# Storing the split of layer one's output weights in DRAM in the second chunk and loading it from there in chunks three to five

## The chip, the cores and the metric

The kernel runs on one core of a Trainium2 chip. The metric is the device time of one execution in microseconds, over the whole kernel from the first instruction to the last output; several runs are taken and their median is quoted.

## What is computed

Three stages, one after the other, in float32 (the sizes are those of the kernel):

```
attention: B, H, S, D = 4, 8, 576, 64, causal window of 128, a linear bias per head
    attn = softmax(q k^T / sqrt(D) + bias, masked);  x = attn v        -> x is (2304, 512)
layer one: d_ff = 1536
    g = x @ w_gate;  val = x @ w_val
    x = (g * sigmoid(g) * val) @ w_out                                  -> (2304, 512)
layer two: d_ff = 2048
    h = x @ w_in
    y = (h * tanh(softplus(h))) @ w_out                                 -> (2304, 512)
```

The weights of the two layers arrive as raw 64-bit words and are converted to float32 on the chip.

## The kernel before

**Products.** TensorE multiplies in a rounded float32 type. To keep accuracy most operands are split into a rounded part and what is left of it, here called the halves: ScalarE writes the rounded copy (`hi_act`, L123), VectorE the difference (`lo_dve`, L126). A product then takes three matmuls: high by high, high by low, low by high. All matmuls go through `mm` (L116).

**Tokens.** The 2304 tokens of attention and layer one run in five chunks, `A_CHUNKS = [512, 384, 512, 512, 384]`, called `ci` = 0 to 4 in the code and first to fifth in this text. While TensorE computes layer one of a chunk, the attention of the next one is woven in piece by piece. The order on TensorE is the program's order; on the other engines and on SP, whose queue issues nearly all the transfers, a scheduler that models the time sets the order when the kernel is built.

**Layer one.** For each of 12 blocks `i` of 128 hidden features, `gv_groups` computes gate and value (24 matmuls into `g_ps`, operands `xt` and `w`) and splits the result into `hh` and `hl`; `out_group` then adds the block's product with the output weights (12 matmuls into four accumulators `acc`, through `proj`). The output product of a block runs one block after its gate and value; in the fifth chunk it lags six blocks (`lastlag`), so the last seven blocks' output products follow each other directly at the end of layer one.

**The ring.** The output weights of two blocks, 128 x 1024 numbers, make one piece `r` (six pieces for a chunk). In use it lies as halves, 128 x 2 x 1024, in a `ring` tile; there are two such tiles (`ring_tile`, `bufs=2`). The first chunk converts the raw words (`conv_ring`) and writes the float32 weights to DRAM (`w1od`). For every later chunk `load_ring(ci, r)` is called when the output product of the piece two before it has been issued, so that the tile just used can be filled again. It puts four steps at the front of the list `bg` of background steps: load 512 KB from `w1od` into a `cw` tile, an empty step, ScalarE's high half and VectorE's low half. `pump` takes a few steps from that list after each group of TensorE's work, and `need` forces those that are due.

**Other background work on the same list.** `conv_w2` converts layer two's 16 weight blocks in the second to fourth chunk (raw words into the one `wraw` tile; ScalarE's L434 makes `cg`; VectorE's L446, L439, L451 and L460 make `cw`; then a store to `w2d`). In the fifth chunk `combos` loads eight of these blocks from `w2d` (`cw`), forms differences on GpSimd (`ct`, L577), splits them into `chl` and writes them to `w2o` (16 stores). `make_win` prepares layer two's input weights (`w` from `w2d`, differences `t` on GpSimd at L850, halves `win`).

**Layer two.** It runs three times over 768 tokens: products into `bk` from `xs` and `win`, then from `op` and `wout` (loads of 1024 KB from `w2o`).

Of the kernel before, what the change touches and what calls it, by code (L numbers as in the profile page):

```python
# [9 lines left out]
F32 = mybir.dt.float32  # L10
# [12 lines left out]
NF1, NF2 = F1 // 128, F2 // 128  # L23
# [70 lines left out]
def body(ctx: ExitStack, tc: tile.TileContext, qT, kT, vP, w1, w1o, w2, cst, yT):  # L94
    nc = tc.nc
# [6 lines left out]
    dr = ctx.enter_context(tc.tile_pool(name="dr", bufs=1, space=bass.MemoryType.DRAM))  # L102
# [2 lines left out]
    x2d = dr.tile([128, CT, NT], F32, name="x2d")  # L105
    w1od = dr.tile([NF1 // 2, 128, 1024], F32, name="w1od")
    w2d = dr.tile([NF2, 128, 1024], F32, name="w2d")
    w2o = dr.tile([7, 128, NJ, 2, 256], F32, name="w2o")
    cst_sb = const.tile([128, 452], F32, name="cst_sb")
    nb = {128: cst_sb[:, 0:128], 0: cst_sb[:, 128:256]}  # L110
# [290 lines left out]
    wt, ring, spill = {}, {}, {}  # L401
    bg = collections.deque()
    done = set()
# [16 lines left out]
    def steps(key, fs, front=False):  # L420
        if front:
            bg.extendleft([(key if f is fs[-1] else None, f) for f in fs][::-1])
            return
        for f in fs[:-1]:
            bg.append((None, f))
        bg.append((key, fs[-1]))
# [39 lines left out]
    def halves(st, alloc, put):  # L466
        def f1():
            st["h"] = alloc()
            hi_act(st["h"][:, 0], st["w"])

        def f2():
            lo_dve(st["h"][:, 1], st["w"], st["h"][:, 0])
            put(st["h"])

        return [f1, f2]

    def ring_tile():
        return hp_.tile([128, 2, 1024], F32R, tag="ring", name="ring", bufs=2)
# [46 lines left out]
        )  # L525

    def load_ring(ci, r):
        st = {}

        def f0():  # L530
            st["w"] = hp_.tile([128, 1024], F32, tag="cw", name="cw")
            nc.sync.dma_start(out=st["w"], in_=w1od[r])

        def put(w):
            ring[ci, r] = w

        steps(
            ("ring", ci, r), [f0, lambda: None] + halves(st, ring_tile, put), True
        )
# [177 lines left out]
    def out_group(ci, i):  # L717
        p = plansA[ci]

        def o():  # L720
            acc = get_acc(("A", ci))
            hh, hl = hs.pop(("A", ci, i))
            r, j = divmod(i, 2)
            need(("ring", ci, r))
            proj(acc, p.n, ring[ci, r], 512 * j, hh, hl, i == 0, i == NF1 - 1)
            if j == 1:
                ring.pop((ci, r))
                if ci == 0 and r + 2 < NF1 // 2:
                    conv_ring(r + 2)
                else:  # L730
                    nxt = (ci, r + 2) if r + 2 < NF1 // 2 else (ci + 1, r + 2 - NF1 // 2)
                    if nxt[0] < len(plansA):
                        load_ring(*nxt)
            if i == NF1 - 1:
                with tc.high_priority(CFG["evprio"]):
                    evacuate(acc, p.n, x2d[:, :, p.t0:p.t0 + p.n])

        return [o]
# [439 lines left out]
```

## Time and profile before

| | us |
|---|---|
| median of 3 runs (lowest, highest) | 941.27 (940.84, 942.20) |
| the execution that was profiled | 940.25 |
| its span, first to last instruction | 938.4 |
| TensorE busy in it | 917.4 (98%) |
| VectorE, ScalarE, GpSimd busy | 698.2, 518.1, 198.5 |

The profiled execution's own time is its span and 1.85 us around it; it lies 1.02 us under the median. "Busy" of TensorE is the time in which at least one matmul was in its pipeline; the row of weight loads (PEld) runs beside it. A row of the timeline gives the start, the length, the engine, the line, what is written from what, and in brackets how long the engine sat idle before it and what ended that.

### The profile page before, as it was taken

The page shows a single profiled execution, that of the slowest core. Times are in us where ns is not written, and L with a number is a line of the kernel's source. Part 1 is how long each engine was busy: PE and PEld are TensorE (multiplying, and loading weights), DVE is VectorE, ACT ScalarE, POOL GpSimd, SP SyncE. Part 2 cuts the span into 40 slices and gives each one's busy share as a digit, 9 for nine tenths or more (in the row PEclk, how much of TensorE's full clock was granted, in tenths as well). Part 3 has the DMA queues.
Part 4 walks back from the last instruction along what each step waited for, and adds up shares of the span by engine and source line. Part 5 has one row for each costly group of instructions (what it writes and reads, how often), then busy time and mean ns, then how long its engine had stood idle before and what let it go on. Part 6 is the DMA issues. An engine that isn't in the chain of part 4 may idle for free. (4 is left out here: it accounts for less than half of the span.)

```text
span 938.4 us, 14535 instructions
## 1 busy us (share of the span) xinstructions
PE 917.4 (98%) x5016; PEld 820.8 (87%) x5016; DVE 698.2 (74%) x1333; ACT 518.1 (55%) x1127; POOL 198.5 (21%) x332
## 2 busy tenths in 40 slices
PE   5999999999999999999999999999999999999998
PEld 4765678898998888888878999999999999999998
DVE  6898996677866776477664896678976789766874
ACT  6865667656675755355433554564645545455442
POOL 1312132110210332001012455451012410131000
PEclk9999999999999999999999999999999999999999
DMA  9855443366636554164427986625793257930375
GB/s 350 293 216 180 146 125 101 104 212 202 207 106 183 193 175 160 32 208 156 155 100 269 375 292 216 227 90 187 262 299 113 82 187 261 308 119 2 105 260 195
DMA packets 76729, 174.86 MB, mean 186 GB/s; under 512 B 8944, under 2 KB 52336, under 8 KB 66928
## 3 DMA queue, kind: packets, MB, share of 16 engines
q1 hardware_dynamic: 76512, 173.67, 56.1%
q8 instruction: 40, 0.66, 0.3%
q14 instruction: 33, 0.27, 0.1%
q10 hardware_dynamic: 144, 0.26, 0.1%
HBM read 138.25 MB, written 35.65 MB: 185 GB/s over the span
## 5 line engine op out<-in xcount | busy, mean ns | idle before, releaser
L116 PE MATMUL g_ps<-xt,w 128*128 128x512 f32 (+1 forms) x1440 | 318.3, 373 | 0.0
L116 PEld LDWEIGHTS g_ps<-xt,w 128*128 128x128 f32 x1440 | 257.6, 188 | 36.7 <-issue 3.5
L116 PE MATMUL bk<-xs,win 128*128 128x384 f32 x1008 | 175.8, 334 | 1.3 <-DVE G L759 1.0
L116 PE MATMUL bk<-op,wout 128*128 128x384 f32 x1008 | 175.8, 334 | 0.9 <-DMA wout<-w2o 0.8
L116 PEld LDWEIGHTS bk<-xs,win 128*128 128x128 f32 x1008 | 174.7, 188 | 1.9 <-DVE G L759 1.3
L116 PEld LDWEIGHTS bk<-op,wout 128*128 128x128 f32 x1008 | 174.8, 188 | 1.5 <-issue 1.5
L116 PE MATMUL acc<-hh,ring 128*128 128x512 f32 (+1 forms) x432 | 132.3, 369 | 0.1
L123 ACT ACTIVATE op<-G 128x768 fp32r<-128x768 f32 x84 | 71.1, 847 | 64.3 <-PE bk L116 54.4
L280 POOL TENSOR_SCALAR_AFFINE_SELECT PT<-PT 128x256 f32<-128x256 f32 (+4 forms) x80 | 44.2, 568 | 232.2 <-ACT PT L277 232.0
L126 DVE TENSOR_TENSOR op<-G,op 128x768 fp32r<-128x768 f32 x84 | 79.5, 957 | 15.8 <-ACT op L123 15.0
L116 PEld LDWEIGHTS acc<-hh,ring 128*128 128x128 f32 x432 | 80.0, 188 | 10.0 <-DVE ring L126 0.4
L850 POOL TENSOR_TENSOR t<-w 128x256 f32<-128x256 f32 x48 | 40.2, 858 | 209.6 <-DVE win L126 146.7
L116 PE MATMUL acc<-hl,ring 128*128 128x512 f32 (+1 forms) x216 | 79.0, 366 | 0.0
L759 DVE TENSOR_TENSOR G<-u,bk 128x384 f32<-128x384 f32 x72 | 39.7, 553 | 41.4 <-PE bk L116 39.8
L249 ACT ACTIVATE Pt<-Pt,sm 128x128 f32<-128x128 f32 (+1 forms) x160 | 62.3, 391 | 14.0 <-DVE sm L245 13.3
L686 ACT ACTIVATE t<-g_ps 128x512 f32<-128x512 f32 (+1 forms) x60 | 32.9, 548 | 48.5 <-PE g_ps L116 48.3
L123 ACT ACTIVATE hh<-t 128x512 fp32r<-128x512 f32 (+1 forms) x54 | 31.3, 579 | 45.3 <-DVE t L702 45.1
L687 DVE SCALAR_TENSOR_TENSOR t<-t,g_ps 128x512 f32<-128x512 f32 (+1 forms) x60 | 37.6, 627 | 22.9 <-ACT t L686 22.9
L1122 ACT ACTIVATE G<-G 128x384 f32<-128x384 f32 x72 | 37.2, 517 | 29.0 <-DVE G L759 29.0
L264 ACT ACTIVATE Pt<-Pt,sm 128x128 f32<-128x128 f32 (+1 forms) x144 | 46.3, 391 | 9.2 <-DVE sm L260 9.0
L702 DVE SCALAR_TENSOR_TENSOR t<-t,g_ps 128x512 f32<-128x512 f32 (+1 forms) x54 | 33.6, 623 | 20.1 <-PE g_ps L116 19.1
L126 DVE TENSOR_TENSOR hl<-t,hh 128x512 fp32r<-128x512 f32 (+1 forms) x54 | 36.5, 676 | 16.0 <-ACT hh L123 15.2
(84 smaller groups left out, 1266.9 us busy)
## 6 DMA issues: line engine op xcount, KB each, us to landing
wout<-w2o SPq DMA_DIRECT2D x42, 1024.0 KB, 5.9
wraw<-w SPq DMA_DIRECT2D x16, 1024.0 KB, 5.5
w2o<-chl SPq DMA_DIRECT2D x16, 896.0 KB, 8.8
wst<-w SPq DMA_DIRECT2D x12, 1024.0 KB, 7.8
cw<-w1od SPq DMA_DIRECT2D x24, 512.0 KB, 4.5
w<-w2d SPq DMA_DIRECT2D x24, 512.0 KB, 3.5
w2d<-cw SPq DMA_DIRECT2D x16, 512.0 KB, 4.7
wraw<-w1o SPq DMA_DIRECT2D x6, 1024.0 KB, 6.8
```

What stands on the lines that cost most here:

```text
L116: nc.tensor.matmul(out=out, lhsT=lhsT, rhs=rhs, start=start, stop=stop, skip_group_check=True)
L123: return nc.scalar.activation(out=out, in_=in_, func=AF.Copy)
L126: return nc.vector.tensor_tensor(out=out, in0=in_, in1=hi.bitcast(F32), op=ALU.subtract)
L249: last_of["sum"] = nc.scalar.activation(out=Pt[:q.qn], in_=Pt[:q.qn], func=AF.Exp, scale=-1.0, bias=sm[:q.qn, i:i + 1], accum_out=sm[:q.qn ...
L264: last_of["exp"] = nc.scalar.activation(out=pt, in_=pt, func=AF.Copy, scale=r)
L280: nc.gpsimd.affine_select(out=here, in_=prev, pattern=[[0, m], [1, n]], compare_op=ALU.is_ge, fill=0.0, base=0, channel_multiplier=-1,)
L686: tanhs.append(nc.scalar.activation(out=t[:, :n], in_=st["g"][:, :n], func=AF.Tanh, scale=0.5))
L687: nc.vector.scalar_tensor_tensor(out=t[:, :n], in0=t[:, :n], scalar=1.0, in1=st["g"][:, :n], op0=ALU.add, op1=ALU.mult)
L702: nc.vector.scalar_tensor_tensor(out=t[:, :n], in0=t[:, :n], scalar=0.5, in1=vps[:, :n], op0=ALU.mult, op1=ALU.mult)
L759: last_of["add"] = nc.vector.tensor_tensor(out=out, in0=a, in1=b, op=op)
L850: nc.gpsimd.tensor_tensor(out=x[:, o], in0=a, in1=b, op=ALU.subtract)
L1122: nc.scalar.activation(out=out, in_=in_, func=AF.Mish)
```

## The change

`load_ring` of the second chunk also stores each piece's halves to a new DRAM tensor `w1oh` (six stores of 1024 KB), right after VectorE has written the low half. For the third to fifth chunk `load_ring` no longer adds steps to the list: it takes a `ring` tile and issues one load of 1024 KB from `w1oh` straight into it, and ScalarE and VectorE split nothing. Line numbers behind the new lines are 1, 6 or 7 higher.

```diff
@@ -105,6 +105,7 @@
     x2d = dr.tile([128, CT, NT], F32, name="x2d")
     w1od = dr.tile([NF1 // 2, 128, 1024], F32, name="w1od")
     w2d = dr.tile([NF2, 128, 1024], F32, name="w2d")
+    w1oh = dr.tile([NF1 // 2, 128, 2, 1024], F32, name="w1oh")
     w2o = dr.tile([7, 128, NJ, 2, 256], F32, name="w2o")
@@ -525,6 +526,11 @@
     def load_ring(ci, r):
+        if ci >= 2:
+            ring[ci, r] = ring_tile()
+            nc.sync.dma_start(out=ring[ci, r].bitcast(F32), in_=w1oh[r])
+            done.add(("ring", ci, r))
+            return
         st = {}
 
         def f0():
@@ -533,6 +539,7 @@
 
         def put(w):
             ring[ci, r] = w
+            nc.sync.dma_start(out=w1oh[r], in_=w.bitcast(F32))
 
         steps(
             ("ring", ci, r), [f0, lambda: None] + halves(st, ring_tile, put), True
```

The scheduler's order on TensorE and on GpSimd is the same in both kernels. The order moves on SP, ScalarE and VectorE, from the second chunk to the end of layer one. Two places of it follow.

**SP, the end of the fifth chunk, before.** `cw<-w1od` are the old loads of the output weights, `cw_...<-w2d` and `w2o<-chl` the loads and stores of `combos`, `w_...<-w2d` the weights for `make_win`, `x2d<-ev` the results of layer one.

```order
L612 DMA w2o<-chl 128x7x256 x2
L532 DMA cw<-w1od 128x1024
L588 DMA cw_5839<-w2d 128x1024
L612 DMA w2o<-chl 128x7x256
L843 DMA w_5854<-w2d 128x1024
L612 DMA w2o<-chl 128x7x256 x2
L532 DMA cw<-w1od 128x1024
L612 DMA w2o<-chl 128x7x256
L843 DMA w_5905<-w2d 128x1024
L612 DMA w2o<-chl 128x7x256
L666 DMA x2d<-ev 128x2x384 x2
```

The last two loads of output weights stand ahead of five and of two of the sixteen `w2o` stores.

SP, the same stretch, with the change:

```order
L531 DMA ring<-w1oh 128x2048
L619 DMA w2o<-chl 128x7x256
L595 DMA cw_5749<-w2d 128x1024
L619 DMA w2o<-chl 128x7x256 x2
L531 DMA ring<-w1oh 128x2048
L850 DMA w_5816<-w2d 128x1024
L619 DMA w2o<-chl 128x7x256 x2
L850 DMA w_5867<-w2d 128x1024
L619 DMA w2o<-chl 128x7x256
L531 DMA ring<-w1oh 128x2048 x2
L673 DMA x2d<-ev 128x2x384 x2
```

Each load into `ring` now waits for TensorE to be done with the tile, so it stands where that comes: the third piece behind ten stores, the fourth behind thirteen, the fifth and sixth together behind all sixteen.

**ScalarE, the middle of the second chunk, before.** `cg<-wraw` is the conversion of a weight block that has to be loaded first; `K` and `Q` are the split of the next head's keys and queries, `ring<-cw` the high half of an output weight piece.

```order
L686 ACTIVATE t<-g_ps 128x384
L249 ACTIVATE Pt,sm<-Pt,sm 128x128 x2
L434 ACTIVATE cg<-wraw 128x1024
L123 ACTIVATE K_2518<-kraw 128x640
L203 ACTIVATE Q<-qraw 128x512
L123 ACTIVATE hh<-t 128x384
L249 ACTIVATE Pt,sm<-Pt,sm 128x128 x2
L123 ACTIVATE ring<-cw 128x1024
L277 ACTIVATE PT<-t_ps 128x4x128
```

The conversion stands ahead of `K` and `Q`.

ScalarE, the same place, with the change:

```order
L693 ACTIVATE t<-g_ps 128x384
L250 ACTIVATE Pt,sm<-Pt,sm 128x128 x2
L124 ACTIVATE K_2523<-kraw 128x640
L204 ACTIVATE Q<-qraw 128x512
L124 ACTIVATE hh<-t 128x384
L250 ACTIVATE Pt,sm<-Pt,sm 128x128 x2
L278 ACTIVATE PT<-t_ps 128x4x128
L265 ACTIVATE Pt<-Pt,sm 128x128 x4
L435 ACTIVATE cg<-wraw 128x1024
```

`K` and `Q` stand ahead of the conversion now.

## Rows read from the trace of the kernel before

**Rows 1.** The page's head and its busy times by engine.
```profile
span 938.4 us, 14535 instructions
PE 917.4 (98%) x5016; PEld 820.8 (87%) x5016; DVE 698.2 (74%) x1333; ACT 518.1 (55%) x1127; POOL 198.5 (21%) x332
```

**Rows 2.** Busy times by stretch: second, third, fourth, fifth chunk, layer two.
```profile
core 0: us, PE busy (x) PEld busy (x) DVE busy (x) ACT busy (x) POOL busy (x), PEclk, DMA share, GB/s
183.00:285.00 102.00, 100.26 (x637) 94.39 (x636) 76.00 (x194) 66.33 (x183) 17.89 (x38) 1.00 0.62 188
285.00:405.00 120.00, 120.00 (x635) 97.58 (x634) 78.21 (x190) 67.15 (x188) 23.21 (x56) 1.00 0.48 150
405.00:512.00 107.00, 107.00 (x535) 87.36 (x534) 69.29 (x131) 49.36 (x104) 13.84 (x22) 1.00 0.51 167
512.00:584.00 72.00, 71.63 (x411) 70.98 (x410) 59.59 (x70) 37.84 (x55) 35.36 (x36) 1.00 0.86 300
584.00:937.00 353.00, 349.15 (x2009) 347.93 (x2008) 264.26 (x353) 175.24 (x272) 66.16 (x85) 1.00 0.54 181
```

**Rows 3.** What TensorE waited for from 100 us on: total, times, longest.
```profile
PE s_ps L116 <- DVE Q L205: 3.2, 4, 1.3
PE bk L116 <- DVE G L759: 1.0, 1, 1.0
PE bk L116 <- DMA wout<-w2o: 0.8, 1, 0.8
PE bk L116 <- DVE ev L665: 0.3, 1, 0.3
```

**Rows 4.** All instructions that write `ring`: ns shortest, median, longest.
```profile
L123 ACT ACTIVATE ring<-cw x27: 1042/1057/1064, 98.6 to 574.6; 128x1024 fp32r<-128x1024 f32 x27
L126 DVE TENSOR_TENSOR ring<-cw,ring x27: 1184/1226/1760, 99.7 to 576.0; 128x1024 fp32r<-128x1024 f32 x27
```

**Rows 5.** Timelines of the second chunk: SP, ScalarE, VectorE, TensorE.
```profile
223.53 0.38 SPq L491 DMA_DIRECT2D wraw<-w  x1
...
230.30 1.13 ACT L434 ACTIVATE cg<-wraw 128x1024 bf16<-128x1024 bf16 x1 [3.08 <-DMA wraw<-w]
231.33 0.72 ACT L123 ACTIVATE K<-kraw 128x640 fp32r<-128x640 f32 x1
...
232.94 0.69 DVE L205 SCALAR_TENSOR_TENSOR Q<-qraw,Q 64x512 fp32r<-64x512 f32 x1
...
233.69 0.38 PE L116 MATMUL s_ps<-K,Q 128*128 128x256 f32 x1 [1.35 <-DVE Q L205]
```

**Rows 6.** TensorE's timeline, fifth chunk: output products, then layer two.
```profile
535.76 0.35 PE L116 MATMUL acc<-hh,ring 128*128 128x384 f32 x1
542.03 0.35 PE L116 MATMUL acc<-hh,ring 128*128 128x384 f32 x1
567.10 0.35 PE L116 MATMUL acc<-hh,ring 128*128 128x384 f32 x1
573.53 0.34 PE L116 MATMUL acc<-hl,ring 128*128 128x384 f32 x1
573.97 0.62 PE L116 MATMUL acc<-hh,ring 128*128 128x384 f32 x2
581.89 0.34 PE L116 MATMUL acc<-hh,ring 128*128 128x384 f32 x1
583.55 34.60 PE L116 MATMUL bk<-xs,win 128*128 128x384 f32 x198 [0.27 <-DVE ev L665]
```

**Rows 7.** ScalarE's and VectorE's timelines: splits of single pieces, fourth and fifth chunk.
```profile
494.20 1.06 ACT L123 ACTIVATE ring<-cw 128x1024 fp32r<-128x1024 f32 x1 [0.99 <-PE acc L116]
...
572.22 1.69 DVE L126 TENSOR_TENSOR ring<-cw,ring 128x1024 fp32r<-128x1024 f32 x1
```

**Rows 8.** Issue to landing of loads of 1024 KB: all of `wout`, all of `wraw`.
```profile
DMA to landing us min/median/max: 4.9/5.9/10.0
DMA to landing us min/median/max: 4.7/5.6/8.8
```

**Rows 9.** Transfers by stretch, KB each, median us to landing: 520 to 540, 556 to 570.
```profile
w2o<-chl SPq DMA_DIRECT2D x5, 896.0 KB, 10.5
w2o<-chl SPq DMA_DIRECT2D x4, 896.0 KB, 7.0
```

**Rows 10.** SP's timeline, end of the fourth chunk and of the fifth.
```profile
492.35 1.26 SPq L588 DMA_DIRECT2D cw<-w2d  x2
...
569.59 0.36 SPq L612 DMA_DIRECT2D w2o<-chl  x1
```

## The prediction

> **What bounds the kernel now.** I read the page's head first, then busy times by stretch, then TensorE's waits, then the timelines at the few places where it waits. TensorE is busy 98% of the span [rows 1]. By stretch the point is sharper: in the third and fourth chunk, 285 to 512 us, it is busy for every microsecond, in the fifth chunk for 71.63 of 72, in the second for 100.26 of 102, always at the full granted clock of 1.00 [rows 2], which is the upper of its two levels. VectorE has free time in all of them: the length less its busy time is 26, 42, 38 and 12 us from the second to the fifth chunk, and ScalarE has more [rows 2]. From 100 us on TensorE lost 5.3 us to named waits [rows 3]: 3.2 for queries that VectorE split late (attention), 0.3 for the results of layer one being copied out, 1.0 and 0.8 in layer two. The kernel is TensorE's work end to end, and the change takes no matmul away: 5016 before, in the same order after. So it can gain only what lies in these waits and can lose wherever a new wait on TensorE appears.
>
> **The change part by part.**
>
> *The splits removed.* Of 27 splits of a piece [rows 4] the change leaves nine (three in the first chunk, six in the second). 18 go: 18 x 1.06 = 19 us of ScalarE and 18 x 1.23 = 22 us of VectorE. Between 285 and 512 us TensorE has no wait that this could end, so twelve of the 18 are worth nothing there. The matmuls are the cover; if it were gone the most would be the 22 us.
>
> *The loads doubled.* 18 loads of 512 KB become 18 of 1024 KB, 9 MB more over some 300 us where the transfers' share is 0.48, 0.51 and 0.86 [rows 2]. The price of one is that of the nearest row of equal size and direction: 5.9 us in the median for `wout`, 5.6 for `wraw`, 4.7 at the least and 10.0 at the most [rows 8]. The load cannot start before TensorE has finished with the tile, since the halves go straight into it; before, only the splits waited for the tile and the 512 KB had been fetched ahead. So each load has the time of one piece's use, two output products and what lies between. In the fifth chunk two such products start 6.27 us apart, at 535.76 and 542.03 [rows 6], so a tile has 12.5 us, and 10.0 fits. In the chunks with 512 columns it has more. These loads cost nothing, with the other tile's work as cover.
>
> *The end of the fifth chunk is the exception.* There seven output products run back to back: 84 matmuls from 567.10 to 582.06 [rows 6], which is the last one's start at 581.89 and the 0.17 that one takes, less the pause at 573.97, which is 2.10 us for a product and 4.2 for a piece. The third piece is used up with the first of the seven, at 569.2; the fifth piece's load can start then, and TensorE wants it two products on, at 573.4. Before, the splits took 1.06 and 1.7 us there and ended only a little late: TensorE paused 0.26 us, from 573.71 to 573.97, for a low half that VectorE wrote from 572.22 to 573.91 [rows 6, 7]. Now a load has to land in those 4.2 us, less the wake-up of SP and that of TensorE: from the end of that split to TensorE's start it was 0.06 us, and twice that is 0.1 (an estimate). So TensorE waits for the landing time less about 4.0. At 4.7 that is 0.7, at 10.0 it is 6.0. I take 5.9, since `wout` is the same shape on the same route: **1.9 us**. The median is nearer than the slow end, because the last `w2o` stores should be out before this load: SP issued the sixteenth at 569.59 [rows 10], with three splits fewer ahead of it on VectorE, and landings late in the chunk have come down from 10.5 to 7.0 [rows 9]. The sixth piece's load starts at 573.4, lands at 579.4 by the same row, and is wanted at 573.4 + 1.9 + 4.2 = 579.5: no second wait at that landing time.
>
> The Trainium skill, "DMA: Bandwidth & Descriptors", section "Anatomy of one DMA — SWDGE (gpsimd) path", fits a transfer as 2.0 us and the bytes at 436 GB/s, so 1 MiB in 4.4 us (an estimate from that page, whose fit is for another issuing path than SP's). By it the wait would be 0.4 us and the kernel 1.5 us faster than in my sum; the fastest such load here took 4.7 [rows 8], so I stay with the rows.
>
> *Waits that go there.* The 0.26 us pause goes with its split, and the wait of 0.27 us at 583.55 for VectorE's copies [rows 6] goes too, since VectorE has two splits less ahead of them while TensorE arrives later. Together −0.5.
>
> *The steps taken off the list.* Each of the 18 loads took four steps of the list; without them the conversion of layer two's weights comes earlier in chunks three and four, where neither engine is full. Nothing for TensorE. At the end of the fourth chunk SP now has three loads into `ring` in a row, and the first two loads of `combos` stand behind them. The third of these waits for a tile that TensorE let go at 494.2 [rows 7], so `combos` starts near 494.5 where it started at 492.35 [rows 10], 2.2 us later, bounded below by 0 and above by the 10.0 of one landing. VectorE's 12 us of room in the fifth chunk and six splits less (7 us) take that up by 569 us; if not, see the first rival.
>
> *SP's queue.* A load that waits for TensorE holds all that stands behind it. In the fifth chunk that is, behind the third piece's load, the last `combos` load and two stores; behind the fourth's, two loads for `make_win`; behind the last two, only results that TensorE has not yet computed. All were issued at about these times before, so I put it at nothing, with 2 us for the first of them at the most, the same 2.2 as above.
>
> *The stores in the second chunk.* Six stores of 1024 KB, 6 MB more in 102 us where the transfers' share is 0.62 [rows 2] at 188 GB/s: some 60 GB/s more, share about 0.8. The issue of one takes SP 0.4 us, in front of loads of keys, queries and raw words. Nothing waits for the stores themselves before the third chunk. The price is what they delay.
>
> *The order in the second chunk.* The largest single wait for queries, 1.35 us at 233.69, has its cause on ScalarE: the conversion at 230.30 sat 3.08 us for raw words that SP had asked for at 223.53, and `K` and `Q` stood behind it, so VectorE ended `Q` at 233.6 [rows 5]. With the change `K` and `Q` stand ahead of the conversion, so the wait goes: **−1.35**. Later raw words, by up to the 3 us between the 5.6 and the 8.8 of [rows 8], then hold up a conversion and no query. The bound above is 0 (another head takes its place), the one below −1.7, with all the waits there.
>
> *The sum.* +1.9 − 0.5 − 1.35 = +0.05, so 940.3 on the profiled execution's 940.25. That execution lies 1.02 under the median; on the median's scale it is **941.3**.
>
> **What a measurement tells.** 0.2% is 1.9 us, about what a measurement of this kernel can tell from no change. The forecast is no change.
>
> **The rivals.**
>
> *A crowded landing at the end (slower).* Place: the load of the fifth piece at 569 us. With 9 to 10 us, as loads have it beside others [rows 8, 9], TensorE waits 5 to 6 instead of 1.9 and the kernel takes 944.4 to 945.4. It gets there too if `combos` runs late, since that load stands behind the sixteenth store on SP and every microsecond of that store past 569.2 is one of TensorE. It decides from a landing of 7.7 us on, with the second chunk's gain, or 6.4 without. For it: the share of 0.86 and the three engines' chain in `combos`. Against: the last stores had been issued by 569.59 even with the splits in the way. Chance 0.22.
>
> *The stores crowd the second chunk (slower).* 6 MB more delay the loads of queries and keys, and the 3.2 us of waits for queries grow instead of shrinking. If the 1.35 stays and doubles, the kernel is at 941.3 + 2.7 = 944.0. Against: a share of 0.62 leaves room, and queries are loaded a head ahead. Chance 0.06.
>
> *Relief everywhere (faster).* The last load lands at 4.7, which costs 0.7, all 1.7 of the second chunk's waits for queries go, and the 1.0 that TensorE waits for VectorE in layer two goes [rows 3], with two splits less ahead of layer two's weights: 0.7 − 0.5 − 1.7 − 1.0 = −2.5, 938.8. Against: that wait hangs on a chain that starts from TensorE's own products and moves with it. Chance 0.12.
>
> *The change does not do what it says.* If the new loads waited for the last of the six stores, or were not early in any chunk, TensorE would show waits at every piece, 15 times (landing minus room). The rows of SP show each load into `ring` right where its tile comes free, so I give this no chance of its own beyond the range's edge, 0.02, slower.
>
> **How the numbers follow.** Forecast 0.58; the rivals 0.22, 0.06, 0.12 and 0.02. Slower by over 0.2%: 0.22 + 0.06 + 0.02 = 0.30, of which some lie just inside, so 0.28. Faster 0.12. Within: 0.60. The range runs from 939.5, the forecast with the full 1.7 gained and a landing of 4.7 (1.6 under it), to 945.0, inside the first rival; left out are about half of the faster rival and a third of the slower ones, under 2 in 10.
>
> **What would show it.** Right: 18 splits less, nine left in the rows of `ring`; no wait of TensorE between 285 and 560 us; one new wait, on a transfer into `ring`, of 1 to 3 us near 573 us; the wait for `Q` near 233 us gone; layer two as before, shifted by a microsecond at most. Wrong: waits for `ring` in other places, two of them at the end, a wait for `Q` that has grown, or TensorE held at the start of layer two by `win`.

## The result and the profile after

| | before | after |
|---|---|---|
| median, us (lowest, highest), 4 runs each side by side | 941.74 (940.84, 942.62) | 953.55 (953.31, 955.21) |
| ratio to before, 95% interval | | 1.0124 [1.0102, 1.0145] |
| span of the profiled execution, us | 938.4 | 951.6 |

The change costs 11.8 us. The forecast was 941.3 with a range from 939.5 to 945.0, so the result lies far outside, on the side of the slower rivals and beyond the price of each. The two profiled executions took 940.25 and 953.31, so the traces have 13.1 us to explain and not 11.8.

The page of the kernel after, its head and its busy times by engine, against [rows 1]:

```profile
span 951.6 us, 14475 instructions
PE 920.7 (97%) x5016; PEld 823.3 (87%) x5016; DVE 675.1 (71%) x1315; ACT 502.9 (53%) x1109; POOL 192.1 (20%) x332
```

The 18 splits are gone from both engines: VectorE has 23.1 us less to do, ScalarE 15.2. TensorE has the same 5016 matmuls, and the span is 13.2 us longer. Busy times by stretch in the kernel after, as in [rows 2]:

```profile
core 0: us, PE busy (x) PEld busy (x) DVE busy (x) ACT busy (x) POOL busy (x), PEclk, DMA share, GB/s
183.00:285.00 102.00, 99.61 (x632) 93.79 (x631) 74.73 (x193) 65.38 (x179) 15.31 (x36) 1.00 0.76 243
285.00:405.00 120.00, 116.74 (x617) 94.60 (x617) 67.56 (x175) 59.72 (x175) 15.74 (x59) 1.00 0.52 166
405.00:512.00 107.00, 105.95 (x528) 85.69 (x527) 61.24 (x128) 43.52 (x102) 13.31 (x18) 1.00 0.57 190
512.00:584.00 72.00, 67.66 (x385) 66.87 (x384) 54.27 (x68) 34.60 (x53) 36.30 (x37) 0.99 1.03 358
584.00:937.00 353.00, 351.18 (x2006) 350.25 (x2006) 262.01 (x348) 175.81 (x275) 69.36 (x88) 0.99 0.54 178
```

The third and fourth chunk, where TensorE was busy for every microsecond, now have holes of 3.3 and 1.1 us, although both other engines have less to do there. The fifth has one of 4.3, and its mean granted clock is 0.99. TensorE's waits from 100 us on, against [rows 3] (total, times, longest):

```profile
PE s_ps L117 <- DVE Q L206: 5.6, 6, 1.4
PE acc L117 <- DMA ring<-w1oh: 4.3, 1, 4.3
PE o_ps L117 <- issue: 1.9, 1, 1.9
PE bk L117 <- DMA wout<-w2o: 1.3, 2, 0.8
PE bk L117 <- DVE G L766: 1.0, 1, 1.0
PE g_ps L117 <- DVE sm L246: 0.7, 1, 0.7
```

Matmul for matmul, both traces have the same order on TensorE, so the start of the same matmul can be subtracted. This ledger, worked out from the two traces, is where the 13.2 us of the spans went; "lag" is after minus before:

| where, us in before | first matmul that is later | change of the lag | lag then |
|---|---|---|---|
| second chunk, 208.75, 233.69, 257.90 | `s_ps<-K,Q` | +1.12, -1.41, +0.95 | 0.68 |
| third chunk, 321.41 | `o_ps<-PT,v` | +1.94 | 2.62 |
| third chunk, 345.11, 345.57 | `s_ps<-K,Q`, `g_ps<-xt,w` | +0.85, +0.98 | 4.44 |
| fourth chunk, 435.02 | `s_ps<-K,Q` | +1.31 | 5.75 |
| fifth chunk, 573.36 | `acc<-hh,ring`, the fifth piece | +4.60 | 10.35 |
| 573.53 to 576.86 | its next matmuls, at half the clock | +2.4 | 12.74 |
| start of layer two, 583.55 | `bk<-xs,win` | -0.33 | 12.41 |
| layer two, 928.59 | `bk<-op,wout` | +0.57 | 12.98 |

Two losses hold 12.1 of the 13.2 us: 5.1 in the third and fourth chunk, 7.0 at the end of the fifth. They have different causes. The rest is +0.7 in the second chunk, where the forecast had -1.35, and small changes in layer two.

**The third and fourth chunk.** The conversion of layer two's weights runs closer together. The rows of the `wraw` tile from 285 to 512 us; first the kernel before (of one instruction: shortest, median, longest ns, then first and last start; then what its engines waited for: us, times; then the landings), second the kernel after, where `DVE cw L447` is of those that waited for the tile:

```profile
L446 DVE TENSOR_SCALAR cw<-wraw x11: 684/692/778, 293.2 to 488.3; 128x1024 int32<-128x1024 int32 x11
...
  DMA wraw<-w: 16.6, 8
...
DMA to landing us min/median/max: 4.9/5.3/6.1
```

```profile
L447 DVE TENSOR_SCALAR cw<-wraw x11: 694/694/718, 285.4 to 451.9; 128x1024 int32<-128x1024 int32 x11
...
  DMA wraw<-w: 30.6, 14
...
  DVE cw L447: 10.0, 7
...
DMA to landing us min/median/max: 5.1/6.6/9.4
```

Of eleven passes the last starts at 452 us instead of 488. There is one tile for raw words, so the next load starts only when the passes before it are over; closer passes wait more often, 14 times instead of 8, and now on VectorE too, 10.0 us in seven waits, where it had none. What such a wait does to TensorE shows at 321 us. From the timelines of SP, ScalarE, VectorE and TensorE of the kernel after, with the wait ahead of an instruction in brackets:

```profile
310.53 0.33 SPq L492 DMA_DIRECT2D wraw<-w  x1
...
319.49 1.15 ACT L435 ACTIVATE cg<-wraw 128x1024 bf16<-128x1024 bf16 x1 [3.93 <-DMA wraw<-w]
...
319.50 0.69 DVE L447 TENSOR_SCALAR cw<-wraw 128x1024 int32<-128x1024 int32 x1 [4.05 <-DMA kraw<-kT]
...
323.25 0.68 DVE L694 SCALAR_TENSOR_TENSOR t<-t,g_ps 128x512 f32<-128x512 f32 x1
...
324.03 1.75 PE L117 MATMUL o_ps<-PT,v 128*64 128x256 f32 x24 [1.87 <-issue]
```

Both engines stand for 4 us before a pass whose words SP had asked for at 310.53, 9.0 us earlier. (For VectorE's wait the page names a load of keys, which this pass does not read; ScalarE's pass on the same words starts 0.01 us before it.) The work that stands behind the pass on VectorE comes late, among it the product that reads a `g_ps` bank; it ends at 323.93, and 0.10 later TensorE starts the matmuls that need a bank. The page can name no releaser for this wait. (That the bank is what TensorE waited for is read from these times, and was not tried apart.)

**The end of the fifth chunk.** SP's timeline and TensorE's in the kernel after:

```profile
566.50 5.47 SPq L619 DMA_DIRECT2D w2o<-chl  x2
572.13 0.44 SPq L850 DMA_DIRECT2D w<-w2d  x1
572.85 0.86 SPq L619 DMA_DIRECT2D w2o<-chl  x1
575.24 4.50 SPq L531 DMA_DIRECT2D ring<-w1oh  x2
```

```profile
583.71 0.66 PE L117 MATMUL acc<-hh,ring 128*128 128x384 f32 x1 [4.34 <-DMA ring<-w1oh]
584.16 0.52 PE L117 MATMUL acc<-hl,ring 128*128 128x384 f32 x1
...
589.88 0.34 PE L117 MATMUL acc<-hl,ring 128*128 128x384 f32 x1
590.05 0.51 PE L117 MATMUL acc<-hh,ring 128*128 128x384 f32 x2
```

The load of the fifth piece is issued at 575.24, as soon as TensorE has left the tile; TensorE has used up the piece between at 583.71 - 4.34 = 579.37, 4.13 us later. The load's landing time is the longest of the three after 560 us:

```profile
DMA to landing us min/median/max: 6.7/7.3/8.3
```

8.3 less 4.1 is the wait, to 0.2 us. The landing belongs to its stretch: the same loads in the same kernel took 5.3 us in the median between 285 and 512 us, where the transfers' share is 0.52 and 0.57, and 8.3 between 512 and 560. Of the last three `w2o` stores, asked for at 566.50, 571.59 and 572.85, two were still under way at 575.24, the last until 581.86. (That these stores are what slowed the load was not tried apart.)

Then the clock falls; busy times and granted clock in three stretches around it:

```profile
570.00:580.00 10.00, 9.37 (x54) 9.05 (x53) 7.45 (x9) 7.09 (x9) 5.05 (x6) 1.00 1.06 368
580.00:590.00 10.00, 6.29 (x20) 6.32 (x21) 2.65 (x2) 1.06 (x1) 7.08 (x8) 0.66 0.53 209
590.00:600.00 10.00, 10.00 (x60) 10.00 (x59) 2.78 (x5) 1.48 (x3) 0.00 (x0) 1.00 0.47 142
```

From 583.7 to about 589.9 matmuls start 0.32 us apart instead of 0.17, the lower of the two levels of the clock: 2.4 us more.

### The profile page after: what moved, and what is told of

It reads as the page before. It is cut to its first block, busy times and chain, and to the rows that moved or that the text cites. A ratio compares the mean times of both kernels' runs of the same rounds, so it can differ in the third digit from the quotient of the medians.

```text
span 951.6 us, 14475 instructions
## 1 busy us (share of the span) xinstructions
PE 920.7 (97%) x5016; PEld 823.3 (87%) x5016; DVE 675.1 (71%) x1315; ACT 502.9 (53%) x1109; POOL 192.1 (20%) x332
## 4 chain that ended last, share of the span: by engine, by line
PE 78%; DVE 8%; DMA 8%; issue 2%; SPq 2%; ACT 1%; POOL 1%; DVEq 0%; ACTq 0%; POOLq 0%
PE bk L117 34%; PE g_ps L117 25%; PE acc L117 13%; PE s_ps L117 3%; PE o_ps L117 3%; DMA wraw<-w 2%; DMA wout<-w2o 2%; PE t_ps L272 1%; DVE cw L452 1%; DMA v<-vP 1%; DVE Pt L246 1%; DMA ring<-w1oh 1%; DVE cw L447 1%; POOL t L857 1%; SPq L189 1%
## 5 line engine op out<-in xcount | busy, mean ns | idle before, releaser
L117 PE MATMUL acc<-hh,ring 128*128 128x512 f32 (+1 forms) x432 | 134.5, 374 | 4.3 <-DMA ring<-w1oh 4.3
L281 POOL TENSOR_SCALAR_AFFINE_SELECT PT<-PT 128x256 f32<-128x256 f32 (+4 forms) x80 | 39.1, 505 | 238.2 <-ACT PT L278 238.0
```

The source lines that it names most:

```text
L117: nc.tensor.matmul(out=out, lhsT=lhsT, rhs=rhs, start=start, stop=stop, skip_group_check=True)
L281: nc.gpsimd.affine_select(out=here, in_=prev, pattern=[[0, m], [1, n]], compare_op=ALU.is_ge, fill=0.0, base=0, channel_multiplier=-1,)
```

## The experiments

Each ratio is to runs of the kernel before on the same chip in the same session (their medians were 940.2 to 942.4; the changed kernel's own is in the section above). Parts of a loss are read from the ledger of each kernel against the profile of before, made as above. The runs of one kernel scatter by 2 to 9 us, so single profiles can begin a few microseconds late; only the change of the lag inside a stretch is used.

**1. Stores alone.** All chunks load and split as before.

```diff
-        if ci >= 2:
+        if ci >= 5:
...
-            nc.sync.dma_start(out=w1oh[r], in_=w.bitcast(F32))
+            if ci == 1:
+                nc.sync.dma_start(out=w1oh[r], in_=w.bitcast(F32))
```

> Only the six stores of the halves in the second chunk are added to the kernel before; every chunk loads the words and splits them as before, so the list of steps is as it was. Theory 'stores crowd the second chunk': the new waits there (+1.3 near 209 us, +0.9 near 258) come with the stores, the wait at 233.7 goes only if the order on ScalarE changes too; 941.5 to 944. Rival 'all of the second chunk's shift is order': no change, 941.2 to 942.2, and the wait of 1.35 at 233.7 stays.

Measured: 941.36, ratio 1.0016 [1.0000, 1.0032]. The lag changes by +1.58 at 208.75, -1.41 at 233.69 and -0.65 at 257.90; the third to fifth chunk are as before. So the first two moves of the second chunk come with the stores, the gain forecast at 233.69 among them, and nearly cancel. The rival's time holds, its reason (the wait at 233.69 stays) doesn't; of the first theory's two new waits the one near 209 us comes and the one near 258 doesn't.

**2. The list's steps put back.**

```diff
-            done.add(("ring", ci, r))
+            steps(("ring", ci, r), [lambda: None] * 4, True)
```

> Each direct load leaves four empty steps at the head of the list of background steps, as many as the old load had; loads, stores and computation are the changed kernel's. In the changed kernel TensorE's lag against the kernel before grows by 5.1 us in the third and fourth chunk. Theory 'pace': the four steps taken off the list make the conversion of layer two's weights come earlier there, and its wait for raw words on ScalarE holds keys and queries behind it. Then the lag at 512 us falls from 5.8 to about 0.7, and the time from 953.5 to about 948.5. Theory 'SP held' (a load that waits for its tile holds the loads of queries, keys and raw words queued behind it on SP): nothing changes in those chunks, 952.5 to 954.5.

Measured: 954.03, ratio 1.0141 [1.0116, 1.0167]; +4.66 in the third and fourth chunk. It looks like a verdict for "SP held", but the edit did not do what it was for: the order on VectorE stays that of the changed kernel. The table counts how many of VectorE's products for hidden units (`t<-t,g_ps`, 24 to a chunk, the third from 48, the fourth from 72 to 96) stand ahead of each conversion pass in its order:

| kernel | third and fourth chunk's eleven passes |
|---|---|
| before | 46 49 52 56 60 70 72 76 80 84 86 |
| after; after with the steps | 44 46 49 50 52 68 70 72 74 75 76 |
| after with a `cw` tile (run 4) | 44 46 49 52 56 68 70 72 74 76 80 |
| after with tile and steps (run 5) | 45 48 52 56 60 70 72 76 80 84 86 |
| after with held passes (run 3) | 46 50 54 58 62 68 70 74 78 80 84 |

**3. The passes held.**

```diff
-                raw["f"][k]()
+                held = blocks[0] != shares[0][0]
+                with tc.issue_after(last_of["hl"].ins) if held else ExitStack():
+                    raw["f"][k]()
```

> The changed kernel, with each pass of layer two's conversion in the third and fourth chunk held behind the low half of hidden units that stands before it in the program. That puts the passes back to about the spacing they have before (one block per four or so hidden units, the last in unit 84 instead of 76). Theory 'dense conversion': waits for raw words on VectorE and ScalarE and TensorE's waits at 321, 346 and 435 us go, lag at 512 us about 0.7 instead of 5.8; 948 to 949. Theory 'SP held': the loads that wait for a tile in SP's queue still hold queries, keys and raw words; lag at 512 us stays at 4 to 6 and the time at 952 to 954.

Measured: 950.64, ratio 1.0110 [1.0076, 1.0143]. TensorE is busy for 120.00 of 120 us in the third and 107.00 of 107 in the fourth chunk, and the lag doesn't change between 285 and 512 us:

```profile
285.00:405.00 120.00, 120.00 (x642) 97.92 (x641) 71.48 (x188) 63.01 (x188) 20.75 (x64) 1.00 0.54 172
405.00:512.00 107.00, 107.00 (x531) 86.60 (x530) 63.17 (x131) 43.71 (x104) 11.93 (x18) 1.00 0.55 184
```

That is the first theory in the trace; the direct loads, still in SP's queue, hold no query there. The time is 1.6 us above what was expected, and by the time alone this run could not be told from the changed kernel (1.0124 [1.0102, 1.0145]). The profiled execution is the slowest of its four, 955.73: it lost 7.2 us before 285 us (waits for `Q` of up to 2.2 us and two stretches at half clock), and the tail cost 4.97 + 2.1.

**4. A tile of `cw` for each direct load.** The words had held such a tile from their load until the split, and `conv_w2` takes its `cw` from the same two.

```diff
+            w = hp_.tile([128, 1024], F32, tag="cw", name="cwx")
+            nc.gpsimd.memset(w[:, :1], 0.0)
             ring[ci, r] = ring_tile()
+            nc.vector.tensor_copy(out=ring[ci, r][:, 0, :1], in_=w[:, :1])
```

> The changed kernel, in which each direct load also takes a tile of cw, as the words did: one column is set by GpSimd, and VectorE copies it into the ring tile before the load, so the cw tile is kept until TensorE has left the ring tile. Theory 'shared tile': the words held a cw tile and by that spaced the conversion; the passes go part of the way back (the last in unit 80 instead of 76, 84 to 86 before), and 2 to 5 of the 5 us come back in the third and fourth chunk; the tail stays, 948 to 951. Rival 'work on the engines': the spacing came from the splits' own time; then the waits at 321, 346 and 435 us stay, 953 to 955.

Measured: 954.01, ratio 1.0135 [1.0112, 1.0158]: a miss for the first theory, and the rival's time without its waits: those at 321 and 346 us go. A new one stands at 435 us in the times of before, 3.4 us for `Q` with 1.3 of half clock behind it:

```profile
436.80 0.69 DVE L447 TENSOR_SCALAR cw<-wraw 128x1024 int32<-128x1024 int32 x1 [3.66 <-DMA w2d<-cw]
...
440.62 0.58 PE L117 MATMUL s_ps<-K,Q 128*128 128x256 f32 x1 [3.37 <-DVE Q L206]
```

By the page VectorE stands there until a store from `cw` has landed and the pass has a tile to write to. So the edit moves the passes part of the way back and brings a wait of its own.

**5. Tile and steps together.** The edits of runs 2 and 4 in one kernel.

> The changed kernel with both things that the old loads had beside their splits: a tile of cw held until TensorE has left the ring tile, and four (empty) steps at the head of the list. With either alone the conversion stayed dense; with both, its passes stand at the places they have before (the last in unit 86). Theory 'the conversion was spaced by the tile and the steps together': the third and fourth chunk are full again, lag at 512 us 0.5 to 2 instead of 5.8, the tail's 7 us stay, 947 to 949.5. Rival 'the splits' own work mattered, or the larger loads delay raw words whatever the order': 2 us or more of waits stay in those two chunks, 950 to 954.

Measured: 951.43, ratio 1.0090 [1.0063, 1.0117], 9.1 us over its own session's 942.36, 1.9 above the range in absolute time. Busy times of the third and fourth chunk:

```profile
285.00:405.00 120.00, 120.00 (x640) 97.88 (x639) 72.56 (x195) 62.97 (x188) 22.31 (x70) 1.00 0.54 172
405.00:512.00 107.00, 107.00 (x533) 86.75 (x532) 63.14 (x135) 44.79 (x104) 13.97 (x24) 1.00 0.56 188
```

Both are full again, and the lag is 6.35 at either end (the clock was at 0.86 between 20 and 100 us of this profile, which is most of it). Raw words land no sooner than in the changed kernel (6.4 us in the median and 8.0 at the most, against 6.6 and 9.4), yet VectorE no longer stands before a pass for them. So the old loads spaced the conversion by two things together, the tile they held and the four steps each; the change took away both. The splits' own work was not needed for it. The tail loses 6.1 us here, in two waits, 1.9 for `hl` with half clock behind it and 2.5 for the load of the fifth piece.

**6. Room at the end of the fifth chunk, first try.** The fifth piece goes into two `cw` tiles, asked for with the fourth; the sixth takes the tile that the third leaves.

```diff
+        if ci == 4 and r >= 3:
+            for k in {3: (3, 4), 4: (5,), 5: ()}[r]:
+                direct(ci, k)
+            return
```

> In the fifth chunk the fifth piece goes into two tiles of cw that nothing uses by then, and is asked for right behind the fourth; the sixth goes into the tile that the third leaves, one piece earlier than in the changed kernel. No load of this chunk now has less than two pieces' time. Theory 'room': the wait of 4.3 us and the stretch at half clock go, 953.5 - 7.0 = 946.5. Rival 'crowding': the landings late in the chunk grow with three loads behind one another and the 16 stores, one load still comes late, 949 to 953.

Measured: 950.00, ratio 1.0093 [1.0064, 1.0123]: the rival's outcome. The fifth piece is in time, the sixth is not. Its load is issued at 576.14 and TensorE waits for it:

```profile
587.24 0.41 PE L117 MATMUL acc<-hh,ring 128*128 128x384 f32 x1 [2.81 <-DMA ring<-w1oh]
```

The longest landing into `ring` after 560 us is 11.0 us. 2.97 of lag and 1.5 of half clock replace 4.6 and 2.4.

**7. The fifth chunk put back, the rest as changed.**

```diff
-        if ci >= 2:
+        if 2 <= ci < 4:
```

> The fifth chunk alone is put back: it loads 512 KB words and splits them, as before; the third and fourth chunk keep the direct loads, the second its stores. Theory 'tail': of the 11.8 us lost, 4.6 are TensorE's wait for the load of the fifth piece near 573 us and 2.4 the stretch at half clock behind it; both go and the time is 953.5 - 7.0 = 946.5. Rival 'late third stage': TensorE's lag and the late weights of layer two hold it somewhere else near the end, and only part of this comes back, 949 to 953.

Measured: 949.89, ratio 1.0103 [1.0058, 1.0147]. The wait and the half clock are gone (the lag falls by 0.31 at 574 us), but layer two's first products lose 1.69, 0.68 and 1.19, of which 1.0 comes back by 619 us; the time is the rival's. The edit has a fault: splits of the fifth chunk store their halves again, six stores too many. Run 8 settles what it could not.

**8. Only the last two pieces as words; and the same with held passes.** The first diff alone is run 8a, with that of run 3 it is 8b.

```diff
-        if ci >= 2:
+        if ci >= 2 and (ci, r) < (4, 4):
...
-            nc.sync.dma_start(out=w1oh[r], in_=w.bitcast(F32))
+            if ci == 1:
+                nc.sync.dma_start(out=w1oh[r], in_=w.bitcast(F32))
```

> The changed kernel with only the last two pieces of the fifth chunk fetched ahead as words and split; nothing is held, so conversion is as dense as in the changed kernel. If the losses add up, 5 to 6 us of the third and fourth chunk stay and the 7 of the tail go: 946 to 948. If the late sums of layer two come to bear on top, 949 to 951.

Measured (8a): 946.81, ratio 1.0059 [1.0042, 1.0075]. TensorE waits for no load into `ring`, and the third and fourth chunk cost +4.63 of lag, as in the changed kernel.

> As the held kernel; in the fifth chunk the first four pieces are loaded directly and only the last two are fetched ahead as 512 KB words and split, so no direct load has to land in the 4.2 us of one piece. Theory 'room': no wait for a load in the fifth chunk, no stretch at half clock; 941 to 943. Rival 'crowding': the splits of the last two pieces or the late sums of layer two cost 2 to 5 us; 943 to 947.

Measured (8b): 942.80, ratio 1.0026 [1.0008, 1.0044]. The third, fourth and fifth chunk are full, which the fifth was not even before:

```profile
285.00:405.00 120.00, 120.00 (x637) 97.67 (x635) 71.46 (x184) 62.02 (x180) 19.99 (x62) 1.00 0.55 174
405.00:512.00 107.00, 107.00 (x535) 87.17 (x534) 61.70 (x126) 43.66 (x101) 14.80 (x22) 1.00 0.58 198
512.00:584.00 72.00, 72.00 (x416) 71.96 (x415) 56.18 (x69) 35.30 (x53) 33.43 (x34) 1.00 0.94 328
```

**9. Held passes, the whole fifth chunk as words.** Runs 3 and 7 together, without the extra stores.

> As the held kernel, and the fifth chunk loads 512 KB words and splits them as before, without stores of halves. Theory 'dense conversion' and 'tail' together: both losses go, 941 to 942.5. Rival 'held combos': SP still stands at the last direct load of the fourth chunk until TensorE leaves its tile, the loads for layer two's sums start 8 us late, and layer two's first weights hold TensorE by 2 to 4 us at its start; 943 to 946.

Measured: 944.24, ratio 1.0034 [1.0024, 1.0044]. Neither loss appears in the trace. The time lies in the rival's range, but not for its reason: the first loads of `combos` are asked for at 489.21 us, not 8 us late, and layer two's start costs nothing. What stays in the trace is the second chunk, +1.62, -1.41 and +0.90.

**10. Direct loads in the fifth chunk alone.**

> Only the fifth chunk loads halves directly; the third and fourth load 512 KB words and split them as before; the second stores the halves. Conversion passes of layer two keep the places they have before. Theory 'two losses': the 5.1 us of the third and fourth chunk do not appear, the wait near 573 us and the half clock behind it do: 4.6 + 2.4 = 7 us over the kernel before, 947 to 949. Rival 'lateness': the load of the fifth piece came late because TensorE and SP were already late by 6 to 8 us, so without that only my 1.9 us of waiting stays, 942 to 943.5.

Measured: 949.47, ratio 1.0094 [1.0062, 1.0125], 8.6 us over its session's 940.87 and 0.5 above the first theory's range. The third and fourth chunk change the lag by nothing; the fifth by +4.65 and 1.5 of half clock:

```profile
580.75 0.66 PE L117 MATMUL acc<-hh,ring 128*128 128x384 f32 x1 [4.46 <-DMA ring<-w1oh]
```

"Lateness" fell: with TensorE only 2.7 us late the load of the fifth piece lands just as slowly (8.5 the longest) and the wait is the same.

**11. Is a faster version in it?** Passes held in the second chunk too, with the last two pieces as words; and, as a control, the kernel before with its passes held.

> As the kernel with held passes and the last two pieces fetched as words, with the passes of the second chunk held too. What is left of the loss lies in the second chunk (+1.05 near 209 us, -1.41 near 234, +1.83 near 258). Theory 'the second chunk's rest is order on VectorE': with the passes behind the hidden units the waits for queries there go, and the time is that of the kernel before or 1 to 2 us under it, 939.5 to 941.5. Rival 'stores': later landings of raw words and of keys hold queries in any order, 941.5 to 944.

Measured: 943.29, ratio 1.0030 [1.0014, 1.0045].

> The kernel before with its passes held in the same way in all chunks, without stores or direct loads: the control for the run above. If holding alone takes the second chunk's 3.2 us of waits for queries, 938 to 940, and the direct loads add nothing to it. If it only pushes the conversion late (its last block now stands in unit 92, in layer two's way), 942 to 946.

Measured: 951.29, ratio 1.0107 [1.0090, 1.0125]. Where the words still take a `cw` tile, holding pushes the last pass to the 92nd product and 511.9 us. TensorE then loses 4.7 us in the fifth chunk to hidden units (`t`) that come late, 4.1 at its end to splits and half clock, and 5.5 in layer two's first products, where one wait alone is 2.84. In the second chunk the control takes 1.5 us off at 233.69 and gives nothing back there; with the stores a wait of 2.0 us at 236 us (ScalarE's `PT`), and a stretch at half clock behind it, takes the same gain away. That asked for one more run: the kernel before with the passes of the second chunk alone held.

> The kernel before with its conversion passes held behind the hidden units in the second chunk alone; no stores of halves, no direct loads, and the passes of the third and fourth chunk at their old places. The control lost nothing in the second chunk and gained 1.7 us at 233.7. If the forecast's -1.35 is there to be had without the stores, the lag falls by 1.4 to 1.7 near 234 us and nothing gives it back: 0.15 to 0.2% under the kernel before. If the gain is given back by other waits, as with the stores, no change.

Measured: 941.17 against 941.71, ratio 1.0000 [0.9986, 1.0013]. The lag falls by 1.5 at 233.69, near the forecast's term, and rises by 0.65 at 257.90. A gain of 0.85 us is below what the runs can show.

**12. Both remedies by other means.** Tile and steps (run 5) with the last two pieces as words.

> As the run above, with the last two pieces of the fifth chunk fetched ahead as words and split, as before. If both causes are named rightly, nothing is left but the second chunk's +0.5 to +1.5: 940.5 to 943. If a third loss hides behind the two, 943.5 or more.

Measured: 944.14, ratio 1.0025 [1.0007, 1.0042]; 1.8 us over its session's 942.36, though in absolute time it is 1.1 above the range and on the side of a third loss. The two chunks are full; one wait of 1.4 us for a load into `ring` stands near 570 us, its landing 10.5; why that one is late was not looked into.

**The sum of it.** By the ratios, the changed kernel's 1.24% falls to 0.59% when the tail goes (6.1 us) and to 0.26% or 0.25% when the spacing comes back as well (3.1 us, by two different edits). The traces put these two at 7.0 and 5.1; the intervals of the ratios are 2 us to either side, so the trace's 5.1 is not excluded. Where the spacing alone is put back and the tail stays, the ratios fall by 1.3 us (run 3) and 3.2 (run 5), with intervals as wide: the size of 5.1 us rests on the traces. The last 0.26%, 2.4 us, was not taken apart; the stores alone are at 0.16%, and in 8b TensorE waits 4.6 us for `Q` where it waited 3.2 [rows 3]. No version beats the kernel before.

## Why the prediction was wrong

**The step that failed first: "The steps taken off the list. … Nothing for TensorE."** It was 5.1 us in the trace. The text had seen that the conversion "comes earlier in chunks three and four" and priced that by how busy the engines are. A wait at the head of an engine's order doesn't ask how busy the engine is: one pass that stands 4 us for raw words holds the work behind it for 4 us, and TensorE had 100% to lose. The second half of the oversight is that only the steps were counted. Each old load also held one of two `cw` tiles that the conversion needs (run 5 needed both, tile and steps, to put the order back).

**The term that was mis-sized: "I take 5.9 …: 1.9 us" at the end of the fifth chunk.** The formula held to a tenth: landing less about 4.0, with 4.13 measured, one wait and no second. The landing was 8.3 instead of 5.9, so the wait 4.3. The reason for 5.9, that "the last `w2o` stores should be out before this load", failed: the last is issued 2.4 us before the load and lands 9.0 us later, the share of the transfers is 1.06 in 570 to 580 us, and run 10 shows the same landing without the earlier lag. The row of `wout`, 5.9, was taken in layer two, where all its 42 loads stand and the share is 0.54 [rows 2]. The rival "a crowded landing" had the mechanism and the place. The Trainium skill, "DMA: Bandwidth & Descriptors", section "Anatomy of one DMA — SWDGE (gpsimd) path", gives 4.4 us for 1 MiB (an estimate from its fit, for another issuing path than SP's). The traces do not agree here: this load took 8.3.

**A term that was missing:** 2.4 us at half clock behind that wait. TensorE had been at 1.00 from the second chunk to the end in the kernel before [rows 2], so the rows showed no price for a long pause.

**A term that the sum had at nothing:** the stores' effect in the second chunk. "The order in the second chunk, -1.35" came at its place, -1.41, but two other waits took the gain (+1.12, +0.95; with the stores alone +1.58 and none). The chunk as a whole is at +0.7, outside the bounds of -1.7 and 0 that the text gave.

**What held.** "Waits that go there, -0.5": 0.25 to 0.31 near 574 us in runs 7, 8a and 8b, and 0.33 at 583.55 in the changed kernel. The other 17 of the 18 loads cost TensorE nothing, as forecast. `combos` starts 8.1 us later, at 500.41 for 492.35 [rows 10], which is the forecast's 2.2 and the 5.84 by which TensorE itself is late there: SP stands until TensorE lets a tile go. Layer two took it: in run 8a, where `combos` starts at 503.10 and TensorE is 8.5 late, its first products wait for nothing. In the working, 1.6 under 941.3 is 939.7 and not 939.5; nothing hangs on it.

## What to carry to other kernels

A step that is taken away gives back not only its work but what it held: a tile of a shared pool and its places in a list, and these may have been what spaced another stream; look at the order of that stream before pricing them at nothing. In an order that an engine must keep, an operation that waits for a transfer is priced by the wait and what stands behind it, not by the engine's free time. A load that goes straight into the tile in use has only the time of the other tile: take the slow end of the landings where transfers are busiest, and fetch the last ones by another way.

## What was not expected of the hardware

The granted clock of TensorE fell to the lower of its two levels around a pause, and the work behind the pause ran at it for a while, with matmuls 0.32 us apart instead of 0.17. This cost 2.4 us after a wait of 4.3 (changed kernel), 1.5 after 4.5 (run 10), 2.1 after 4.8 (run 3) and 1.5 after 2.8 us (run 6). It is no function of the wait's length alone: after the 1.87 at 324 us of the changed kernel, and after one of 2.5 near 586 us in run 5, it stayed at 1.00, while the wait of 1.89 at the same place as the first, 325 us in run 6, and one of 1.9 at 578 us in run 5 were each followed by about 1.5 us of loss. What decides between these was not tried.
